# Sums of the hidden quarters rearranged and partly moved from GpSimd to VectorE, with folds at set places, in a Strassen-like channel block beside attention

## The chip, the cores and the metric

The kernel runs on one core of a Trainium2 chip. The metric is the device time of one execution in microseconds (us); lower is better. Three executions of the kernel before took 1725.05 to 1727.2 us, median 1726.35. All runs in this document are in the fast state.

## The reference, cut to what matters

```python
# attention: 8 batches x 8 heads, 576 positions, head dimension 64
scores = q @ k.T / 8
attn = softmax(where(scores >= max(scores) - tau, scores, -1e9))
x = attn @ v                                  # then (batch, 576, 512)
# Fourier mixing and channel block
u  = x + real(fft(fft(x, axis=1), axis=2))
un = (u - mean(u)) / sqrt(var(u) + 1e-6)
out = u + relu(un @ w_ch1) @ w_ch2            # 512 -> 2048 -> 512
```

## The kernel before

TensorE's order is written by hand. Attention's steps and pieces of the channel block alternate on it, so that the block fills the time in which a softmax runs on VectorE and ScalarE. The order of the other engines comes from a scheduler.

The channel block takes 16 groups of 256 tokens "in quarters": each layer is a 2x2 block product in seven products instead of eight, at the price of sums of blocks. The groups alternate between two orders of products, "up" (even) and "down" (odd). For the output layer the hidden activations `h` lie in four quarters `(i, k)`. I write h00, h01, h10, h11, where h01 is `quarter(1, 0)` and h11 is `quarter(1, 1)`, as in the kernel. Each quarter is 128 x 1024 and is worked on in two parts of 512 columns. These are the sums of `h`:

```python
def s_form(out_, in0, in1, op):              # None stands for s_tile
    for part in range(2):
        ...
        nc.gpsimd.tensor_tensor(out=place[0], in0=place[1], in1=place[2], op=op)
...
if up:
    s_form(None, (1, 0), (1, 1), ALU.add)            # s = h01 + h11
    s_form((1, 0), (0, 0), (1, 0), ALU.subtract)     # h01 := h00 - h01
else:
    s_form(None, (1, 0), (1, 1), ALU.add)
    s_form((1, 0), (0, 0), (1, 0), ALU.subtract)
    s_form(None, None, (0, 0), ALU.subtract)         # s := s - h00
sum_ = bank()
yield from product(sum_, a[0][0], b00, True)         # first product: h00
...
yield from fifth() if up else seventh()              # second: s (up) or h00 - h01 (down)
... # third: h10; fourth: s (up: changed once more); then the other three
```

The hidden layer ends with adds and relus; the last of them are in `third` or `fifth`:

```python
def relu(to):
    nc.scalar.activation(out=to, in_=to, func=ACT.Relu)
...                                    # end of a down group, part 1
    add(h01, y)                        # VectorE
    relu(h01)                          # ScalarE
    add(h11, y)
    relu(h11)
```

Beside this, every pair of heads that attention has finished is "folded" for the Fourier transform: two sums `half`, four sums into `f`, two tiny ones, and after some pairs two wide sums. GpSimd folds the first three pairs of a batch, and VectorE the last, whose result the transform of that batch waits for. The program calls one piece of a fold per attention step (`fold_more`).

Names in the profile lines below: `sc` are attention's scores, `neg` their maxima, `e` the exponentials; `pw` and `pe` are TensorE's transposes of `e`, `e_t` and `ends` ScalarE's copies of these; `py` and `pa` are the two products of the Fourier transform, `y_e` the copy of a part of `py`; `ph` and `po` are products of the hidden and the output layer, `hs` is `h`, `s_tile` is s.

Of the kernel before, what the change touches and what calls it, by code (L numbers as in the profile page):

```python
# [12 lines left out]
ALU = mybir.AluOpType  # L13
ACT = mybir.ActivationFunctionType
# [33 lines left out]
def kernel(  # L48
# [12 lines left out]
    nc = tc.nc  # L61
# [109 lines left out]
    for u in range(2):  # L171
# [10 lines left out]
        out=q_scale[:], in0=tau_t[:], scalar1=0.0, scalar2=SCALE, op0=ALU.is_ge, op1=ALU.mult  # L182
# [3 lines left out]
        out=below[:], in0=tau_t[:], scalar1=0.0, scalar2=-3.0e38, op0=ALU.is_lt, op1=ALU.mult  # L186
# [3 lines left out]
        out=tau_pos[:], in0=tau_t[:], scalar1=0.0, scalar2=-1.0, op0=ALU.max, op1=ALU.mult  # L190
# [697 lines left out]
    def hidden_in_quarters(g, rows, quarter):  # L888


        c0 = tokens_of(g)[0] % RING
        c1 = (c0 + 128) % RING
        up = (g - FIRST) % 2 == 0
        b = [[[u_t[:, 2 * k + c, z : z + 128] for c in range(2)] for z in (c0, c1)]
             for k in range(2)]
        t1, t2, minus_t4 = ([t_u[:, m, c, :] for c in range(2)] for m in range(3))

        def sums(out_, in0, in1):
            for c in range(2):
                nc.gpsimd.tensor_tensor(out=out_[c], in0=in0[c], in1=in1[c], op=ALU.subtract)  # L900

        sums(t1, b[0][1], b[0][0])
        sums(t2, b[1][1], t1)
        sums(minus_t4, b[1][0], t2)

        def weights(eng, part, in0, in1, op=ALU.subtract):
            cols = slice(512 * part, 512 * part + 512)
            for c in range(2):
                eng.tensor_tensor(
                    out=s_u[c][:, cols], in0=in0[c][:, cols], in1=in1[c][:, cols], op=op  # L910
                )

        OPERANDS = {
            1: (a_w1[0][0], b[0][0]), 2: (a_w1[0][1], b[1][0]), 3: (s_u, b[1][1]),
            4: (a_w1[1][1], minus_t4), 5: (s_u, t1), 6: (s_u, t2), 7: (a_w1[1][0], b[0][1]),
        }
        banks = {}

        def product(m, part):
            name = "sum" if m in (1, 6, 7) else m  # L920
            if m not in (6, 7):
                banks[name] = ps.tile([128, 512], FP32, tag="mm", bufs=4, name="ph")
            left, right = OPERANDS[m]
            for q in range(4):
                for c in range(2):
                    nc.tensor.matmul(  # L926
                        banks[name][:, 128 * q : 128 * q + 128],
                        left[c][:, 512 * part + 128 * q : 512 * part + 128 * q + 128], right[c],
                        start=q == 0 and c == 0 and m not in (6, 7), stop=c == 1,
                        skip_group_check=True,  # L930
                    )
            return banks[name][:, :]

        def add(to, bank, other=None):
            nc.vector.tensor_tensor(  # L935
                out=to, in0=bank, in1=to if other is None else other, op=ALU.add
            )

        def relu(to):
            nc.scalar.activation(out=to, in_=to, func=ACT.Relu)  # L940

        def fifth(part):
            y = product(5, part)
            h01, h11 = quarter(1, 0, part), quarter(1, 1, part)
            if up:
                nc.scalar.copy(h11, y)

                weights(nc.gpsimd if part else nc.vector, part, s_u, a_w1[0][0])
            else:
                add(h01, y)  # L950
                relu(h01)
                add(h11, y)
                relu(h11)

        def third(part):
            y = product(3, part)
            h01 = quarter(1, 0, part)
            if up:
                add(h01, y)
                relu(h01)  # L960
            else:
                nc.scalar.copy(h01, y)
                weights(nc.gpsimd, part, a_w1[1][1], a_w1[1][0])

        def first(part):
            nc.scalar.copy(quarter(0, 0, part), product(1, part))

        def second(part):
            h00 = quarter(0, 0, part)
            add(h00, product(2, part))  # L970
            relu(h00)

        def others(part):
            h10, h01, h11 = quarter(0, 1, part), quarter(1, 0, part), quarter(1, 1, part)
            x = product(6, part)
            add(h01, x, h11 if up else None)

            if up:
                weights(nc.vector, part, a_w1[0][1], s_u)
            else:  # L980
                weights(nc.vector, part, s_u, a_w1[0][0], ALU.add)
            yield 4096
            nc.scalar.copy(h10, product(4, part))
            yield 4096
            x = product(7, part)
            add(h10, x)
            relu(h10)
            if up:
                add(h11, x)
                relu(h11)  # L990
            else:
                nc.scalar.copy(h11, x)
            yield 4096

        begin, end = (fifth, third) if up else (third, fifth)
        for one in (first, begin) if up else (begin, first):
            one(0)
            yield 4096
        second(0)
        yield 4096  # L1000
        rows.load(1)

        sums(b[0][1], b[1][1], b[0][1])
        yield ND * 128
        yield from others(0)
        begin(1)
        yield 4096
        rows.load(0)
        yield ND * 128
        for one, part in ((first, 1), (second, 1), (end, 0)):  # L1010
            one(part)
            yield 4096
        rows.factors(0, 2)
        yield from others(1)
        end(1)
        yield 4096
# [35 lines left out]
    def channels_in_quarters(g):  # L1052
# [16 lines left out]
        s_tile = sb.tile([128, size], FP32, tag="sums", bufs=1, name="s_tile")  # L1069
        s_sum = tiles(s_tile)  # L1070

        def s_form(out_, in0, in1, op):

            for part in range(2):
                place = [
                    s_tile[:, 512 * part : 512 * part + 512] if at is None else quarter(*at, part)
                    for at in (out_, in0, in1)
                ]
                nc.gpsimd.tensor_tensor(out=place[0], in0=place[1], in1=place[2], op=op)  # L1079

        def product(bank, left, right, start):
            for p in range(NK):
# [10 lines left out]
        def alone(left, right, *to):  # L1093
            po = bank()
            yield from product(po, left, right, True)
            for t, cols in to:
                rows.add(t, cols, po[:, 0 : DM // 2])
            yield 4 * DM
# [6 lines left out]


        if up:
            s_form(None, (1, 0), (1, 1), ALU.add)
            s_form((1, 0), (0, 0), (1, 0), ALU.subtract)
        else:  # L1110
            s_form(None, (1, 0), (1, 1), ALU.add)
            s_form((1, 0), (0, 0), (1, 0), ALU.subtract)
            s_form(None, None, (0, 0), ALU.subtract)
        sum_ = bank()
        yield from product(sum_, a[0][0], b00, True)
        rows.add(0, LEFT, sum_[:, 0 : DM // 2])
# [16 lines left out]
        else:  # L1133
            combine(t_sum_2, b11_2, t_sum_2)
            s_form(None, None, (0, 0), ALU.add)
        yield from alone(a[0][1], b11, (0, RIGHT))
        if up:
            rows.store(0)
        yield from product(sum_, a[1][1], minus_t4, False)
        rows.add(1, LEFT, sum_[:, 0 : DM // 2])  # L1140
        yield 4 * DM
        yield from seventh() if up else fifth()
        if not up:
            rows.store(0)
        rows.store(1)


    mixes = []
# [61 lines left out]
    folds = []  # L1210
# [62 lines left out]
    def fold_more():  # L1273
        if folds and next(folds[0], True):
            folds.pop(0)
# [89 lines left out]
    while folds:  # L1365
        fold_more()

    by_hand.close()
    ctx.enter_context(tc.manual_schedule(engines={mybir.EngineType.PE}))

    for i in range(2 * per_batch, total + 1):
        if i < total:
            scores(i)
            softmax(i)

        n, t = divmod(i, NT)
        fold_more()
        nothing = iter(())
        prep = prep_in_parts(n + 1) if t == 3 and n + 1 < B * NPAIR else nothing
        weights = weights_in_parts(i - 1)  # L1380
        next(prep, None)
        fill()
        next(weights, None)
        fill()
        next(weights, None)
        next(prep, None)
        fill()
        next(prep, None)
        if t == 2:
            weighted_values(n, 0)  # L1390
        if t == 0:
            weighted_values(n - 1, 1)
            folds.append(fold_rows(n - 1))
            if n % NPAIR == 0:
                while folds:
                    fold_more()
            if n + 1 < B * NPAIR:
                load_v(n + 1)
        if i % per_batch == 0:
            start_batch(i // per_batch - 1)  # L1400
# [49 lines left out]
```

## Time and profile before

| | kernel before |
|---|---|
| median of 3 runs | 1726.35 us |
| span of the profiled run | 1723.9 us |
| TensorE busy, whole span | 95% |
| TensorE idle after 430 us, where the groups in quarters run | 48 us of 1294 |
| of that, waits for GpSimd's difference | 14.9 us in three waits |
| clock granted to TensorE after each of these waits | 0.50 for 6.8 us |

TensorE is the bound. What other engines do matters only where TensorE waits for them. A wait costs its idle time and, where the clock record shows a drop after it, half of the busy time at half clock: the eight matmuls of one output product took 3.78 us there (1065.65 us) and 1.89 us at full clock (1058.37 us).

### The profile page before, as it was taken

The numbers are of one execution on the slowest core, as the hardware profiler recorded it, in microseconds if no ns is written. First come the engines' busy times: TensorE is split into PE (matmuls) and PEld (weight loads), VectorE is DVE, ScalarE is ACT, GpSimd is POOL, SyncE is SP. The second block draws the span as 40 slices with busy tenths as digits, with TensorE's granted clock in tenths as the row PEclk, the third lists the DMA queues.
The fourth block names the chain that finished last, engine by engine and source line by source line (L and its number), as shares of the span: only waits on it lengthen the run. The fifth ranks groups of instructions, "written<-read, shape, count | busy, mean of one in ns | idle before, by whom it ended". The sixth has DMA issues, their size and how long they took to land.

```text
span 1723.9 us, 28923 instructions
## 1 busy us (share of the span) xinstructions
PE 1643.3 (95%) x10838; PEld 1282.9 (74%) x10838; DVE 1128.3 (65%) x2470; ACT 844.9 (49%) x1833; POOL 650.8 (38%) x827
## 2 busy tenths in 40 slices
PE   8998899999999999999999998999989998999998
PEld 4555555576886788788889787777868777889998
DVE  6885885566757676856576757685767757663444
ACT  5863675544454454545345455454636455442111
POOL 5773562042421452334351244224232244235343
PEclk9999999999999999999999999999999999999999
DMA  5313222100010001000010010101001010000000
GB/s 160 112 51 106 70 71 54 31 16 21 22 34 19 23 15 41 22 27 20 15 29 27 22 31 4 41 22 34 15 15 40 22 30 5 13 1 13 13 13 13
DMA packets 130384, 57.48 MB, mean 33 GB/s; under 512 B 121123, under 2 KB 121125, under 8 KB 130246
## 3 DMA queue, kind: packets, MB, share of 16 engines
q1 hardware_dynamic: 128854, 55.35, 11.9%
q8 instruction: 86, 1.41, 0.4%
q14 instruction: 52, 0.43, 0.1%
q10 hardware_dynamic: 1392, 0.30, 0.1%
HBM read 46.02 MB, written 9.44 MB: 32 GB/s over the span
## 4 chain that ended last, share of the span: by engine, by line
PE 72%; DVE 13%; ACT 7%; POOL 4%; issue 2%; DMA 1%; SPq 1%; ACTq 0%; DVEq 0%; POOLq 0%
PE ph L926 22%; PE po L1083 18%; PE pv L589 9%; PE sc L433 6%; PE pw L560 5%; PE po L848 3%; ACT e L469 3%; DVE neg L461 3%; DVE e L477 2%; PE sc L444 2%; PE ph L822 1%; PE py L692 1%; DVE hs L1044 1%; DVE f L673 1%; PE pa L709 1%
## 5 line engine op out<-in xcount | busy, mean ns | idle before, releaser
L461 DVE TENSOR_REDUCE neg<-sc 128x1 f32<-128x576 f32 x288 | 205.7, 750 | 201.4 <-PE sc L433 189.4
L469 ACT ACTIVATE e<-sc,neg 128x576 f32<-128x576 f32 x288 | 211.8, 735 | 250.9 <-DVE neg L461 250.2
L477 DVE SCALAR_TENSOR_TENSOR e<-sc,thr,e 128x576 f32<-128x576 f32 x288 | 227.1, 813 | 59.0 <-ACT thr L473 58.1
L1083 PE MATMUL po<-w,hs 128*128 128x256 f32 x1024 | 248.4, 386 | 0.8 <-DVE u L804 0.6
L1083 PEld LDWEIGHTS po<-w,hs 128*128 128x128 f32 x1024 | 187.3, 191 | 34.3 <-issue 11.5
L926 PE MATMUL ph<-u_t,w 128*128 128x128 f32 x1536 | 187.8, 276 | 0.9 <-DVE hs L935 0.7
L560 PE MATMUL pw<-ident,e 128*128 128x128 f32 x1152 | 170.7, 275 | 15.4 <-ACT ends L552 3.2
L926 PEld LDWEIGHTS ph<-u_t,w 128*128 128x128 f32 x1536 | 178.7, 192 | 6.0 <-issue 1.9
L433 PE MATMUL sc<-kT,qT 64*128 64x288 f32 x1024 | 165.9, 429 | 7.9 <-DVE e L477 7.3
L562 ACT COPY e_t<-pw 128x512 f32<-128x512 f32 x256 | 148.2, 592 | 45.6 <-PE pw L560 44.2
L560 PEld LDWEIGHTS pw<-ident,e 128*128 128x128 f32 x1152 | 135.2, 141 | 34.7 <-issue 4.7
L935 DVE TENSOR_TENSOR hs<-ph,hs 128x512 f32<-128x512 f32 x160 | 107.2, 685 | 82.2 <-PE ph L926 58.1
L433 PEld LDWEIGHTS sc<-kT,qT 64*128 64x128 f32 x1024 | 91.4, 186 | 68.4 <-issue 42.1
L804 DVE SCALAR_TENSOR_TENSOR u<-po,rstd,u 128x256 f32<-128x256 f32 (+1 forms) x164 | 76.2, 483 | 85.5 <-PE po L1083 83.6
L926 PE MATMUL ph<-t_u,s_w 128*128 128x128 f32 x1024 | 126.1, 276 | 1.9 <-ACT ends L548 1.1
L926 PEld LDWEIGHTS ph<-t_u,s_w 128*128 128x128 f32 x1024 | 119.3, 192 | 5.8 <-issue 2.3
L1083 PE MATMUL po<-hs,s_tile 128*128 128x256 f32 x512 | 123.1, 384 | 0.0
L940 ACT ACTIVATE hs<-hs 128x512 f32<-128x512 f32 x128 | 79.1, 629 | 70.5 <-DVE hs L935 70.4
L1079 POOL TENSOR_TENSOR s_tile<-hs 128x512 f32<-128x512 f32 x32 | 42.3, 1323 | 171.4 <-ACT hs L940 158.6
L1083 PEld LDWEIGHTS po<-hs,s_tile 128*128 128x128 f32 x512 | 94.1, 191 | 13.8 <-issue 2.1
L496 ACT ACTIVATE e<-e,den 128x576 f32<-128x576 f32 x96 | 74.4, 775 | 53.0 <-DVE den L489 52.4
L1079 POOL TENSOR_TENSOR hs<-hs,s_tile 128x512 f32<-128x512 f32 x32 | 44.8, 1400 | 127.3 <-PE po L1083 122.6
(196 smaller groups left out, 2979.1 us busy)
## 6 DMA issues: line engine op xcount, KB each, us to landing
hs<-in_moe_w_ch_dram SPq DMA_DIRECT2D x23, 512.0 KB, 4.2
out_dram<-u SPq DMA_DIRECT2D x36, 256.0 KB, 2.1
qk_in<-in_q_dram SPq DMA_DIRECT2D x64, 128.0 KB, 2.2
v_in<-in_v_dram SPq DMA_DIRECT2D x64, 128.0 KB, 2.4
qk_in<-in_k_dram SPq DMA_DIRECT2D x31, 128.0 KB, 2.4
w<-in_moe_w_ch_dram SPq DMA_DIRECT2D x6, 512.0 KB, 7.8
qk_in<-in_k_dram SPq DMA_DIRECT2D x31, 64.0 KB, 2.3
stage<-in_moe_w_ch_dram SPq DMA_DIRECT2D x3, 512.0 KB, 3.7
```

The source lines that it names most:

```text
L433: nc.tensor.matmul(sc[j][:, c, 0:HALF], qT[hp, 128 * t : 128 * t + 128], kT[hp, HALF * c : HALF * (c + 1)], start=True, stop=True,)
L461: nc.vector.tensor_reduce(out=neg[:, j : j + 1], in_=sc[j][:, :, 0:HALF], axis=AXIS_XY, op=ALU.max, negate=True,)
L469: nc.scalar.activation(out=ej, in_=sc[j][:, :, 0:HALF], func=ACT.Exp, bias=neg[:, j : j + 1], scale=1.0)
L477: nc.vector.scalar_tensor_tensor(out=ej, in0=sc[j][:, :, 0:HALF], scalar=thr[:, j : j + 1], in1=ej, op0=ALU.is_ge, op1=ALU.mult, accum_out ...
L560: nc.tensor.transpose(pw[:, c, :], e[:, c0 : c0 + 128], ident[:, :])
L562: nc.scalar.copy(e_t[:, 4 * j : 4 * j + 4, qs], pw[:, :, :])
L589: nc.tensor.matmul(pv[64 * j : 64 * j + 64, 0:m], vt[:, 2 * c + j, :], e_t[:, 4 * j + c, 0:m] if c < 4 else ends[:, 0:m], start=(c == 0), ...
L926: nc.tensor.matmul(banks[name][:, 128 * q : 128 * q + 128], left[c][:, 512 * part + 128 * q : 512 * part + 128 * q + 128], right[c], start ...
L935: nc.vector.tensor_tensor(out=to, in0=bank, in1=to if other is None else other, op=ALU.add)
L940: nc.scalar.activation(out=to, in_=to, func=ACT.Relu)
L1079: nc.gpsimd.tensor_tensor(out=place[0], in0=place[1], in1=place[2], op=op)
L1083: nc.tensor.matmul(bank[:, 0 : DM // 2], left[p], right[p], start=start and p == 0, stop=p == NK - 1, skip_group_check=True,)
```

## The change

The intent is to relieve GpSimd at the end of the hidden layer. In down groups the sum is rewritten: s = h01 + h11 - h00 becomes s = h11 - (h00 - h01), so the difference comes first, on VectorE, and one sum less is left. In up groups the first sum goes to VectorE. The last relu of h01 goes from ScalarE to VectorE. Folds are called at set places of the groups.

```diff
-        def relu(to):
-            nc.scalar.activation(out=to, in_=to, func=ACT.Relu)
+        def relu(to, last=False):
+            if last:
+                nc.vector.tensor_relu(to, to)
+            else:
+                nc.scalar.activation(out=to, in_=to, func=ACT.Relu)
...
-                relu(h01)                       # in fifth (down) and third (up)
+                relu(h01, part == 1)
...
+            background()                        # at five places of a group
...
         if up:
-            s_form(None, (1, 0), (1, 1), ALU.add)
+            s_form(None, (1, 0), (1, 1), ALU.add, nc.vector)
             s_form((1, 0), (0, 0), (1, 0), ALU.subtract)
         else:
-            s_form(None, (1, 0), (1, 1), ALU.add)
-            s_form((1, 0), (0, 0), (1, 0), ALU.subtract)
-            s_form(None, None, (0, 0), ALU.subtract)
+            s_form((1, 0), (0, 0), (1, 0), ALU.subtract, nc.vector)
+            s_form(None, (1, 1), (1, 0), ALU.subtract)
...
+    def background():
+        if late:                                # only after the second batch
+            fold_more()
...
-        fold_more()                             # in each step of attention
+        if t > 2:
+            fold_more()
...
+            while folds:                        # in the step that ends a pair
+                fold_more()
```

More of the change, by code (lines that the diff above doesn't have):

```diff
@@ L959, in third @@
                 add(h01, y)
-                relu(h01)
+                relu(h01, part == 1)
             else:
@@ L1003, in hidden_in_quarters @@
         sums(b[0][1], b[1][1], b[0][1])
+        background()
         yield ND * 128
@@ L1011, in hidden_in_quarters @@
             one(part)
+            if one is second:
+                background()
             yield 4096
@@ L1070, in channels_in_quarters, with s_form @@
         s_sum = tiles(s_tile)
-        def s_form(out_, in0, in1, op):
+        def s_form(out_, in0, in1, op, eng=nc.gpsimd):
             for part in range(2):
@@ L1078, in s_form @@
                 ]
-                nc.gpsimd.tensor_tensor(out=place[0], in0=place[1], in1=place[2], op=op)
+                eng.tensor_tensor(out=place[0], in0=place[1], in1=place[2], op=op)
         def product(bank, left, right, start):
@@ L1136, in channels_in_quarters @@
         yield from alone(a[0][1], b11, (0, RIGHT))
+        background()
         if up:
@@ L1140, in channels_in_quarters @@
         rows.add(1, LEFT, sum_[:, 0 : DM // 2])
+        background()
         yield 4 * DM
@@ L1145, in channels_in_quarters @@
         rows.store(1)
+    def background():
+        if late:
+            fold_more()
+    late = []
     mixes = []
@@ L1366 @@
         fold_more()
+    late.append(True)
     by_hand.close()
```

## The prediction

> **What bounds the kernel now.** I read the page first: the busy shares, the slices and the chain that ended last.
>
> ```profile
> PE 1643.3 (95%) x10838; PEld 1282.9 (74%) x10838; DVE 1128.3 (65%) x2470; ACT 844.9 (49%) x1833; POOL 650.8 (38%) x827
> ...
> PE 72%; DVE 13%; ACT 7%; POOL 4%; issue 2%; DMA 1%; SPq 1%; ACTq 0%; DVEq 0%; POOLq 0%
> ```
>
> TensorE is busy 95% of a span of 1723.9 us, so it is the bound, and any gain must come out of its 80.6 us of idle time or out of stretches where it is busy at a lower clock. No other engine is near its limit, so moving work between VectorE, ScalarE and GpSimd is worth only what it changes in TensorE's waits.
>
> The changed lines are executed only by the groups of the channel block "in quarters". The table of stretches puts TensorE at 1245.6 us busy out of 1294 from 430 us (where these groups start) to the end: 48 us idle there, the other 32 us earlier, where the change does nothing. So I asked for TensorE's waits in that window, and for its groups kept apart by form. First the waits (engine, line, whom it waited for: us in total, times, longest), then the group:
>
> ```profile
> PE po L1083 <- POOL hs L1079: 14.9, 3, 5.0
> PE py L692 <- ACT ends L548: 6.5, 4, 2.1
> PE pw L560 <- ACT ends L552: 3.2, 4, 1.3
> PE pw L560 <- ACT y_e L702: 2.9, 1, 2.9
> PE pa L709 <- ACT e_t L564: 2.7, 4, 0.7
> ```
>
> ```profile
> L1083 PE MATMUL po<-hs 128*128 128x256 f32 x256 | 66.4, 407 | 14.9 <-POOL hs L1079 14.9
> ```
>
> A third of the late idle time is three waits of 5 us, all for one thing: the product of the quarter h01 (left) with t_sum, which waits for GpSimd's difference h00 - h01. In every second group (call it "down") that product, the seventh, comes second in the output layer. The timeline of GpSimd around the first of the three (start, us taken, what) shows why:
>
> ```profile
> 1055.41 1.55 POOL L622 TENSOR_TENSOR half<-x 128x287 f32<-128x287 f32 x2
> 1056.91 1.83 POOL L627 TENSOR_TENSOR f<-half 128x143 f32<-128x143 f32 x4
> ...
> 1059.14 1.48 POOL L651 TENSOR_TENSOR sums<-f 128x608 f32<-128x608 f32 x1
> 1060.57 1.72 POOL L1079 TENSOR_TENSOR s_tile<-hs 128x512 f32<-128x512 f32 x1
> 1062.25 1.91 POOL L652 TENSOR_TENSOR f<-f 128x608 f32<-128x608 f32 x1
> 1064.12 1.47 POOL L1079 TENSOR_TENSOR hs<-hs 128x512 f32<-128x512 f32 x1
> ```
>
> The inputs were done at 1054.8 (h01's relu on ScalarE), but GpSimd ran a pair's fold, then the sum that stands before the difference, then the last fold sum, and ended the difference at 1065.6. TensorE stood from 1060.7 to 1065.65. The other two are the same spot one batch later each (1260.02 and 1454.47).
>
> The wait also costs clock. Stretches around it; the column before the DMA share is the granted clock, the first pair after the comma is the length and TensorE's busy time:
>
> ```profile
> 1060.70:1064.30 3.60, 0.00 (x0) 0.00 (x0) 3.60 (x4) 1.25 (x2) 3.60 (x3) 1.00 0.00 0
> 1064.30:1071.10 6.80, 5.45 (x16) 3.53 (x18) 2.35 (x5) 0.00 (x0) 2.52 (x2) 0.50 0.00 0
> ```
>
> After 3.6 us of idle the clock is 0.50 for 6.8 us, of which TensorE works 5.45 us. The two later spots read 5.68 and 5.83 us at 0.50 and 0.51.
>
> **What the Trainium skill says.** "TensorE: Matmul & The Clock Gate", section "What's actually happening": the clock halves after an idle window of about 3.4 us, the windows run freely, and one busy window brings it back. The trace agrees: two windows (6.8 us) at half clock at each of the three spots, whereas the shorter waits for ScalarE cause one window or none. "GPSIMD Engine Reference", section 3.1: an fp32 elementwise op of two inputs is 1.96x slower on GpSimd than on VectorE. Here it is 1323 to 1527 ns against 684 ns (the median of VectorE's sums of weights, 128x512), 1.9 to 2.2x. The same page, section 1, says that the two share SBUF interfaces; the trace agrees: those VectorE sums run from 665 up to 1893 ns, the long ones beside GpSimd work. "VectorE: DVE Perf Modes", section "Mode 2x_2P", lets an op of one SBUF tensor go at two elements a cycle: the 128x576 scaling of e has a median of 520 ns, so I take 0.46 us for a relu of 128x512 (520 x 512/576).
>
> **The change part by part.** There are 16 such groups, 8 "up" and 8 "down"; every sum comes as two instructions.
>
> 1. In down groups s = h01 + h11 (GpSimd) and s = s - h00 (GpSimd) go; h00 - h01 moves to VectorE; s = h11 - (h00 - h01) stays on GpSimd as one sum. In up groups the first sum h01 + h11 moves to VectorE. GpSimd loses 16 + 16 of the first sum (32 x 1.323 = 42.3 us), 16 differences (16 x 1.429 = 22.9), 16 third sums (16 x 1.527 = 24.4) and gets 16 new ones (16 x 1.32 = 21.1): 68.5 us less. VectorE gets 32 sums, 32 x 0.69 = 22 us when nothing disturbs them.
> 2. The last relu of h01 for part 1 moves from ScalarE (16 x 0.629 = 10 us less) to VectorE (16 x 0.46 = 7.4 us more). VectorE goes from 826 to about 856 us of the 1294, 66%.
> 3. The folds are called at other places of the program. I compared the instruction orders of the two builds. TensorE's is identical. On GpSimd, leaving the sums of h aside, it is identical too, fold for fold; VectorE differs there only in that some sums of weights and adds of h have changed places by one to four positions. So the new fold places move nearly nothing by themselves: in the three bad groups the fold still sits on GpSimd at the same place.
>
> What is on the path: in the three bad groups the seventh product now waits only for VectorE. There the last add of h11 ended at 1055.0 and VectorE then idled 1.09 us until the maxima at 1056.09. The relu (0.46) goes in front of that add, which waited 0.35 us for ScalarE's copy anyway, and the difference (0.69) behind it: done at about 1055.8, some 5 us before TensorE wants it at 1060.7, and the maxima are not put off. So each wait disappears whole.
>
> - Idle removed: 14.9 us (3 x 4.95).
> - Half clock removed: busy time at half clock does half the work, so (5.45 + 5.68 + 5.83) / 2 = 8.5 us.
> - Given back: the product of weighted values comes next. It needs ScalarE's copy of the transposed weights, which started at 1061.95 and took 0.56 us, against TensorE's new arrival at about 1062.6. A residue of 0 to 1 us each, say 0.5 x 3 = 1.5 us.
> - The 48 us of other late waits hang on ScalarE behind the softmax; I count no change there.
>
> Sum: 14.9 + 8.5 - 1.5 = 21.9 us; 1726.35 - 21.9 = 1704.5 us.
>
> **Rivals.** (a) The remaining GpSimd sum takes the wait's place: its second half still stands behind the fold's 1.48 us sum. It would end at about 1062, but the product with s_tile is only the fourth, after 1.9 us of the seventh, 2.8 us of weighted values and the whole third product: not before 1067. Against it: 5 us of margin. If it held, half the gain would go: about 1715. (b) VectorE becomes late: 30 us of new work, all at the end of the hidden layer, right before a softmax whose maxima release ScalarE and then TensorE's transposes. For it: the four waits on ScalarE's ends at L692 come from such a chain, and the longest of them, 2.1 us at 732 us, was followed by a half-clock window. Against it: in up groups VectorE idled 3.5 us before its folds, and in down groups the folds on VectorE took 2.0 us for what takes 0.9 us undisturbed, because GpSimd's sums, now gone, ran beside them. 0.5 us in each group would give 8 us back: 1712. (c) The gaps let other engines catch up, so removing them uncovers other waits soon after. Against it: after the gap ScalarE idled 10.1 us and VectorE 3.3 and 2.9 us in turn, which is slack and not debt. It would leave 1710. (d) More than the three: shorter chains and undisturbed VectorE work also shorten the waits for ScalarE, and with them the three single half-clock windows that the trace's clock record has at 538.7, 569.4 and 733.2 us (3.4 us long, so 1.7 us each at most). That would be 1697 to 1700.
>
> **Range and chances.** The three waits are named, equal in every batch, and their new releaser has 5 us of margin, so the bulk seems safe; (b) and (c) pull up, (d) pulls down. Range 1698 to 1712. Faster by over 2% needs 1691.8 or less, 34.5 us: more than the three waits with their clock and all of (d). Slower by 2% would need VectorE to become the bound at 66%.
>
> **What would show it.** Right: the wait of po for GpSimd's hs is gone from TensorE's waits, the clock is 1.0 past 1060 us with no stretch of 6.8 us at 0.50, TensorE's busy time falls by some 8 us and its idle time by some 14; GpSimd falls by about 68 us, VectorE rises by about 30. Wrong: a wait for GpSimd's s_tile or for VectorE's hs at the output products; waits of ScalarE for the maxima that grow so that those of L692 or L560 pass 3.4 us; or the same waits in TensorE with the time unchanged. If the fold places turn out to matter, the folds would stand elsewhere in GpSimd's timeline than at the 1055 us spot.

## The result, and the profile after

The changed kernel takes 1696.97 us (median of 4 runs, 1695.86 to 1699.09). The ratio to the kernel before is 0.9832, with a 95% interval of 0.9815 to 0.9849. Ratios here are the mean time of one kernel's fast runs over that of the other's in the same rounds, so they are not quite the ratio of the medians quoted. The gain is 29.4 us (1726.35 - 1696.97). The prediction was 21.9 us with a range down to 1698.0, so it was too small by 7.5 us and the result lies 1 us outside the range.

The busy shares and the chain on the page of the kernel after:

```profile
PE 1637.6 (96%) x10838; PEld 1280.9 (75%) x10838; DVE 1137.2 (67%) x2518; ACT 835.4 (49%) x1817; POOL 585.6 (35%) x779
...
PE 75%; DVE 13%; ACT 8%; issue 2%; POOL 2%; DMA 0%; ACTq 0%; DVEq 0%; POOLq 0%
```

TensorE has the same number of instructions, GpSimd fell from 4% to 2% of the chain. TensorE's longest waits from 430 us to the end:

```profile
PE py L692 <- ACT ends L548: 5.3, 4, 1.5
PE pw L560 <- ACT ends L552: 3.2, 4, 1.3
PE pa L709 <- ACT e_t L564: 2.7, 4, 0.7
PE pw L560 <- ACT y_e L702: 2.2, 1, 2.2
```

The 14.9 us for GpSimd's `hs` at the output products are gone. The waits at L692 and for `y_e`, which the prediction left as they were, are shorter too.

The stretch from 430 us to the end, in the kernel before and in the kernel after. Columns are the stretch, its length, then the busy time of TensorE's matmuls, its weight loads, VectorE, ScalarE and GpSimd with their instruction counts, then the granted clock and the DMA share with GB/s:

```profile
430.00:1724.00 1294.00, 1245.56 (x8647) 1038.36 (x8645) 826.36 (x1765) 595.36 (x1270) 459.18 (x547) 0.99 0.08 21
```

```profile
430.00:1697.00 1267.00, 1238.59 (x8662) 1036.35 (x8661) 836.23 (x1814) 587.63 (x1258) 395.88 (x500) 1.00 0.08 22
```

TensorE's idle time fell from 48.4 to 28.4 us and its busy time by 7.0 us. GpSimd fell by 63.3 us. VectorE rose by only 9.9 us although it got 48 more instructions (2470 before, 2518 after, on the two pages).

The spot at 1055 us of the kernel before, now in the kernel after. First GpSimd's timeline (start, us taken), then two stretches around TensorE's product:

```profile
1051.16 1.54 POOL L622 TENSOR_TENSOR half<-x 128x287 f32<-128x287 f32 x2
1052.66 1.84 POOL L627 TENSOR_TENSOR f<-half 128x143 f32<-128x143 f32 x4
...
1054.89 1.48 POOL L651 TENSOR_TENSOR sums<-f 128x608 f32<-128x608 f32 x1
1056.33 1.72 POOL L1086 TENSOR_TENSOR s_tile<-hs 128x512 f32<-128x512 f32 x1
1058.00 1.93 POOL L652 TENSOR_TENSOR f<-f 128x608 f32<-128x608 f32 x1
```

```profile
1050.00:1055.70 5.70, 5.70 (x34) 4.70 (x34) 4.91 (x12) 2.84 (x6) 5.54 (x11) 1.00 0.00 0
1055.70:1063.00 7.30, 7.17 (x46) 4.70 (x45) 7.30 (x10) 1.63 (x4) 4.23 (x3) 1.00 0.00 0
```

The fold stands on GpSimd exactly where it stood. Only the difference is no longer in its queue, and TensorE goes on at full clock.

**Where the time went.** TensorE's order is the same in both kernels, so each of its matmuls can be paired with itself in the other trace. The difference of the two start times, stretch by stretch, is a ledger (times of the kernel before; changes between the two profiled runs):

| stretch, us | change, us | what is there |
|---|---|---|
| 0 to 520 | +1.70 | before the change acts: half-clock windows of the start fall elsewhere |
| 520 to 575 | -3.92 | first down group, with a fold on VectorE |
| 575 to 700 | -0.44 | a wait for qT |
| 700 to 740 | -2.87 | second down group, with a fold on VectorE |
| 740 to 950 | -0.95 | small waits |
| 950 to 1000 | +1.67 | a half-clock window that was not there before |
| 1050 to 1080 | -6.90 | first of the three waits |
| 1080 to 1250 | -0.47 | small waits |
| 1250 to 1275 | -6.98 | second of the three |
| 1275 to 1440 | +1.08 | another new half-clock window, less a small wait |
| 1440 to 1470 | -7.03 | third of the three |
| 1470 to end | -1.03 | small waits |

The sum is -26.1 us; another 0.4 us lie after the last matmul. The profiled runs took 1725.68 and 1699.09 us, the latter the slowest of the four. The three waits brought 20.9 us, close to the 21.9 us predicted. The missing 7 us are in the stretches from 520 to 575 and 700 to 740 (together -6.8 us).

### The profile page after: what moved, and what is told of

It is laid out like the page before. It is cut to its first block, busy times and chain, and to the rows that moved or that the text cites. A ratio compares the mean times of both kernels' runs of the same rounds, so it can differ in the third digit from the quotient of the medians.

```text
span 1697.3 us, 28896 instructions
## 1 busy us (share of the span) xinstructions
PE 1637.6 (96%) x10838; PEld 1280.9 (75%) x10838; DVE 1137.2 (67%) x2518; ACT 835.4 (49%) x1817; POOL 585.6 (35%) x779
## 4 chain that ended last, share of the span: by engine, by line
PE 75%; DVE 13%; ACT 8%; issue 2%; POOL 2%; DMA 0%; ACTq 0%; DVEq 0%; POOLq 0%
PE ph L926 23%; PE po L1090 18%; PE pv L589 9%; PE sc L433 7%; PE pw L560 5%; PE po L848 3%; ACT e L469 3%; DVE e L477 3%; DVE neg L461 3%; PE sc L444 2%; PE py L692 1%; PE ph L822 1%; DVE hs L1051 1%; DVE f L673 1%; PE pa L709 1%
## 5 line engine op out<-in xcount | busy, mean ns | idle before, releaser
L943 ACT ACTIVATE hs<-hs 128x512 f32<-128x512 f32 x112 | 69.3, 629 | 70.9 <-DVE hs L935 70.8
L492 DVE TENSOR_SCALAR e<-e,den 128x576 f32<-128x576 f32 x120 | 81.4, 678 | 2.6
```

The costliest lines, as they stand in the source:

```text
L492: nc.vector.tensor_scalar(out=e[:, 0:S], in0=e[:, 0:S], scalar1=den[:, 0:1], scalar2=None, op0=ALU.mult)
```

## The experiments

My theory after reading the traces had two parts. First, the three waits come from the order of the sums in GpSimd's queue. Second, the 7 us come from VectorE's folds in the first two down groups, which GpSimd's sums no longer slow. Rivals: the fold places; the relief of GpSimd and ScalarE as such; VectorE being the faster engine for the difference. All experiments have the kernel before in the same rounds; its median there was 1726.2 to 1726.4 us.

### e1: the fold places alone

```diff
-        fold_more()
+        if t > 2:
+            fold_more()
         # and background() at its places; sums and relu as before
```

> Only the new places of the folds; sums and relu as before. The build has the same instructions in the same order with the same waits on every engine as the kernel before, so my theory expects 1726 us, ratio 1.000 within the noise of 0.2%. Rival (the fold places carry the 7 us that the prediction missed): 0.996 or less.

Measured: 1726.37 us, ratio 1.0003 (0.9991 to 1.0016). This part of the change does nothing: the scheduler gives the same program. The run is therefore also a measure of the noise. Paired with the profiled run of the kernel before it shows +1.72 us before 430 us and then +0.2 us to the end. So the first 430 us of a run differ by luck, and after that a ledger is good to some tenths of a us.

### e2, e3, e4: the other three parts alone

```diff
 # e2: down groups only
+            s_form((1, 0), (0, 0), (1, 0), ALU.subtract, nc.vector)
+            s_form(None, (1, 1), (1, 0), ALU.subtract)
 # e3: up groups only
+            s_form(None, (1, 0), (1, 1), ALU.add, nc.vector)
 # e4: the last relu only
+                relu(h01, part == 1)
```

> Only the sums of the down groups: difference on VectorE, one sum less on GpSimd; folds, up groups and relu as before. Theory: this carries nearly all. The three waits of 4.95 us and their half clock (20.9 us measured by aligning the two traces) and the faster folds on VectorE at the two early down groups (about 7 us) go: 1726 - 21 - 7 = 1698, ratio 0.982 to 0.986. Rival (relief of GpSimd and ScalarE as such brings the 7 us): only the three waits, 1705, ratio 0.988.

> Only the first sum of the up groups on VectorE (16 instructions). Theory: no wait of TensorE hung on it and no fold of VectorE stands beside it at the spots that matter: ratio 0.998 to 1.001. Rival (GpSimd relief as such): its 21 of the 68 us of relief would bring a third of 7 us, ratio 0.9985 or less; VectorE-late rival: 1.001 to 1.003.

> Only the last relu of h01 on VectorE (16 instructions). Theory: ratio 0.998 to 1.001, since the half us it saves ScalarE is not waited for. Rival (ScalarE relief shortens the waits of the transposes for ScalarE, which were 4 of the 7 us): 0.997 or less.

Measured: e2 1697.55 us, ratio 0.9835 (0.9822 to 0.9849); e3 1719.26 us, 0.9964 (0.9951 to 0.9976); e4 1726.12 us, 1.0002 (0.9988 to 1.0016).

The sums of the down groups alone give all of the gain; relu gives nothing. The up sum alone was a miss: 7 us where my theory expected none. On top of the down sums the medians show no gain (1696.97 against 1697.55), but the ledger of the full change against e2 does: steps of 0.45 to 0.7 us, 2.1 us in all, recur where e3 has them (at 640, 1128, 1315 and 1614 us of e2). A half-clock window at 1335.7 us that e2 does not have (1.6 us) and 0.5 us at 727 us take them back. The ledger of e3 against e1 shows two kinds of things. Some 3.3 us are steps of 0.2 to 0.7 us, several of them at waits for VectorE. Another 2.9 us are two half-clock windows that do not come, although the waits before them are still there. The second kind needs a look. In the kernel before, around the wait of 2.09 us at 732 us:

```profile
729.80:733.20 3.40, 1.31 (x9) 1.13 (x9) 3.02 (x9) 2.65 (x6) 2.03 (x2) 1.00 0.00 0
733.20:736.60 3.40, 3.40 (x13) 2.49 (x12) 2.05 (x6) 1.17 (x3) 0.96 (x1) 0.50 0.00 0
```

And in e3, where the same wait of 2.09 us ends at 733.12 us:

```profile
728.20:731.61 3.41, 2.82 (x16) 2.28 (x14) 3.41 (x7) 0.61 (x3) 2.78 (x1) 1.00 0.00 0
731.61:735.03 3.42, 1.91 (x11) 1.76 (x12) 2.96 (x10) 2.97 (x7) 1.33 (x2) 1.00 0.00 0
```

In each of these traces all half-clock windows start on one grid of 3.413 us, and the stretches above are cut on that grid. In the kernel before, the wait lies within one cell and leaves TensorE busy for 1.31 us of it; the next cell has half clock. In e3 the border of two cells cuts the wait, both cells keep 1.9 us or more of work, and nothing follows. So a shift of some tenths of a us makes or removes 1.7 us. That part of e3 is phase and not relief.

### e5, e6: the down sums in some groups only

```diff
-        else:
+        elif g - FIRST < 5:      # e5; in e6: g - FIRST > 5
             s_form((1, 0), (0, 0), (1, 0), ALU.subtract, nc.vector)
             s_form(None, (1, 1), (1, 0), ALU.subtract)
+        else:
+            ...                  # the three sums of before
```

> The new sums only in the first three down groups (those at about 522, 714 and 871 us), the later five as before. Theory: the three waits for GpSimd stay (14.9 us in the waits), the folds on VectorE at the first two groups go from 3.9 and 4.1 us to about 2.1 and 2.5 us, the waits after them and their half-clock windows go: 7 to 8.5 us less, ratio 0.9950 to 0.9962. Rival (the 7 us is luck of the clock windows or load as such): 0.998 to 1.000.

> The new sums only in the last five down groups, among them the three of the waits. Theory: the three waits with their half clock go and nothing else: 21 us less, 1705, ratio 0.9875 to 0.9885. Rival: with the load spread over all groups, 5/8 of the extra 7 us comes too, 1701, ratio 0.985.

The text for e5 miscounts: the condition holds in the first two down groups (at 522 and 714 us); the one at 871 us has the old sums in both kernels.

Measured: e5 1717.75 us, ratio 0.9952 (0.9940 to 0.9965); e6 1704.08 us, 0.9872 (0.9858 to 0.9885). The gains are 8.7 and 22.4 us, together 31, against 28.7 for e2. The 2 us too many fit clock windows: e5 has only one at the first of the three spots (1.1 us), and e2 has one at 959.4 us that costs 1.7 us. In e5 the ledger against e1 has -7.5 us between 520 and 740 us, and the three waits for GpSimd are still 14.8 us. In e6 it has 7.06, 7.14 and 7.16 us at the three spots and next to nothing elsewhere. The gain sits in five groups: two and three. A relief by the down sums that is spread over all groups is excluded.

### e7: the new order, all on GpSimd

```diff
-            s_form(None, (1, 0), (1, 1), ALU.add)
             s_form((1, 0), (0, 0), (1, 0), ALU.subtract)
-            s_form(None, None, (0, 0), ALU.subtract)
+            s_form(None, (1, 1), (1, 0), ALU.subtract)
```

> Down groups with the difference first and one sum less, all still on GpSimd; VectorE, ScalarE, folds, up groups as before. In the build the difference now stands in front of the fold's big sum. Theory: it ends at about the time TensorE wants it (an estimate of 1060 against 1060.7 us), so the three waits go from 4.95 to under 1 us and the half clock with them; one third of the sums beside the early folds go: 1726 - 20 - 3 = 1703, ratio 0.984 to 0.989. Rival (the gain is VectorE being 2x faster than GpSimd and in no queue behind folds): waits of 2 to 4 us stay, ratio 0.992 to 0.998.

Measured: 1699.03 us, ratio 0.9840 (0.9827 to 0.9854). The full change is 0.9832, within noise. GpSimd's timeline in e7 at the first of the three spots, where TensorE takes the second half of the product at 1055.61 us without a wait:

```profile
1050.48 1.55 POOL L622 TENSOR_TENSOR half<-x 128x287 f32<-128x287 f32 x2
1051.98 0.49 POOL L627 TENSOR_TENSOR f<-half 128x143 f32<-128x143 f32 x1
1052.43 1.28 POOL L1086 TENSOR_TENSOR hs<-hs 128x512 f32<-128x512 f32 x1
```

The difference takes 1.28 us on GpSimd and ends at 1053.7, 1.9 us early. VectorE is not needed for the gain at the three spots (7.9 to 8.0 us each in the ledger): it is enough that no other sum has to come before the difference, so that the scheduler can put it ahead of the fold's wide sum. No run has the difference first and still three sums, so the order and the smaller number of sums are told apart by this timeline only. From 430 us on the ledger puts e7 4.0 us behind the full change (one half-clock window more, and steps of 0.5 to 0.9 us elsewhere); the medians, 2.1 us apart, do not resolve that.

### e8: the old order, the difference on VectorE

```diff
             s_form(None, (1, 0), (1, 1), ALU.add)
-            s_form((1, 0), (0, 0), (1, 0), ALU.subtract)
+            s_form((1, 0), (0, 0), (1, 0), ALU.subtract, nc.vector)
             s_form(None, None, (0, 0), ALU.subtract)
```

> Down groups with the three old sums in the old order, only the difference on VectorE. It overwrites h01, so it must wait for GpSimd's first sum, which stands behind the fold's sum, and VectorE stands in front of the softmax's maxima meanwhile. Theory (order, not engine): waits of about 2 us stay at the three spots, without half clock, VectorE idle up to 7 us before the difference: 15 to 18 us less, ratio 0.989 to 0.992. Rival (engine alone is enough): as the full change, 0.984.

Measured: 1725.74 us, ratio 0.9996 (0.9983 to 1.0008). The engine alone brings nothing, and not even the half that I expected. VectorE's timeline in e8 at the first spot (in brackets the idle time before and who ended it), then TensorE's:

```profile
1061.28 1.93 DVE L1086 TENSOR_TENSOR hs<-hs 128x512 f32<-128x512 f32 x1 [6.87 <-POOL s_tile L1086]
1063.14 1.41 DVE L461 TENSOR_REDUCE neg<-sc 128x1 f32<-128x576 f32 x2
```

```profile
1065.74 1.12 PE L560 MATMUL pw<-ident,e 128*128 128x128 f32 x4 [6.07 <-ACT ends L548]
1066.65 3.62 PE L1090 MATMUL po<-hs 128*128 128x256 f32 x8
```

In VectorE's order the difference stands before the maxima, and VectorE stood 6.87 us before it until GpSimd had read h01. The maxima came at 1063.1. ScalarE's exponentials wait for the maxima, its copy of `ends` stands behind the exponentials, and TensorE's transposes wait for that copy: 6.07 us in place of 4.95. I had expected the late softmax to be hidden; I had overlooked that copy. The wait changed its releaser and its place, and the time stayed.

### e9: VectorE's folds disturbed again

```diff
 # edit of the full change
-            s_form(None, (1, 1), (1, 0), ALU.subtract)
+            for _ in range(3 if g - FIRST < 5 else 1):
+                s_form(None, (1, 1), (1, 0), ALU.subtract)
```

> The full change, but in the first two down groups (at about 522 and 714 us) GpSimd writes its one sum three times over, with the same values each time; nothing waits for the repeats there. Theory (the 7 to 8 us of those two groups are VectorE's folds, slowed by GpSimd sums beside them): the halves go back from 0.53-0.71 to about 1.0 us and the sums of the fold from 0.30 to about 0.56 us each, the maxima come 1.3 to 2 us later, and the waits for ScalarE with their half-clock windows return: 1697 + 5 to 8 = 1702 to 1705, ratio 0.986 to 0.988. Rival (order of the sums, or the number of waits, not contention): 1697 to 1698, ratio 0.983.

Measured: 1702.62 us, ratio 0.9862 (0.9847 to 0.9877), 5.65 us more than the full change. The order on all other engines is that of the full change. VectorE's two groups of folds from 500 to 760 us, in the kernel before, in the full change and in e9 (count, busy us, mean ns of one, then idle time before and its releaser):

```profile
L622 DVE TENSOR_TENSOR half<-x 128x287 f32<-128x287 f32 x4 | 4.0, 1031 | 3.7 <-ACT x L595 3.7
L627 DVE TENSOR_TENSOR f<-half 128x143 f32<-128x143 f32 x8 | 4.0, 563 | 0.0
```

```profile
L622 DVE TENSOR_TENSOR half<-x 128x287 f32<-128x287 f32 x4 | 2.7, 707 | 1.5 <-ACT x L595 1.5
L627 DVE TENSOR_TENSOR f<-half 128x143 f32<-128x143 f32 x8 | 1.9, 295 | 0.0
```

```profile
L622 DVE TENSOR_TENSOR half<-x 128x287 f32<-128x287 f32 x4 | 5.1, 1306 | 1.3 <-ACT x L595 1.3
L627 DVE TENSOR_TENSOR f<-half 128x143 f32<-128x143 f32 x8 | 4.0, 563 | 0.0
```

One repeat follows the other while VectorE folds, and the folds are slower even than before the change: 5.1 + 4.0 us, against 4.0 + 4.0 before and 2.7 + 1.9 in the full change. The maxima come 5.04 and 5.25 us after the start of their scores in the two groups (4.51 and 4.68 before, 2.64 and 3.11 in the full change). The ledger against the full change has +2.83 us between 520 and 545 us, +3.23 us between 700 and 740 us, and -1.67 us for a half-clock window at 960 us that did not come: +4.4 us from 430 us on. (Before 430 us, where the two do the same, e9's profiled run was 4.0 us luckier, so the profiled runs as wholes look alike.) TensorE's wait for `y_e` is back at 2.9 us (2.2 in the full change) and the longest at L692 at 2.1 (1.5). No wait of TensorE for GpSimd came with the repeats. This shows the second part of the theory: GpSimd's sums slow VectorE's folds, the maxima come late, and TensorE waits for ScalarE behind them.

### e10: an attempt at the longest remaining wait

```diff
 # edit of the full change
-                    nc.scalar.copy(y[0:n, u, 256:257], py[0:n, 0:1])
+                    nc.vector.tensor_copy(y[0:n, u, 256:257], py[0:n, 0:1])
```

> The full change, and the copy of one column of y_e (24 instructions) moved from ScalarE to VectorE. It stood behind two exponentials, and TensorE's longest remaining wait (2.18 us at 537 us) hung on it, with a half-clock window after it. Theory: the wait shrinks to under 1 us and the window goes, 2 to 4 us less: 1693 to 1695, ratio 0.980 to 0.982. Rival (the next thing on ScalarE, the copy of ends behind the same exponentials, takes its place, as at L692): 1696 to 1698, ratio 0.983.

Measured: 1702.22 us, ratio 0.9865 (0.9848 to 0.9881), slower than the full change by 5 us. Neither theory had that. From e10's waits of TensorE:

```profile
PE pw L560 <- DVE y_e L702: 6.4, 5, 1.7
```

The copy now stands in VectorE's queue, and TensorE waits for it there, five times in place of once. In return its waits at L692 for `ends` fell from 5.3 to 0.8 us, so the wait changed its place and stayed. From 430 us on, the ledger against the full change adds up to only +0.4 us. The other +2.0 us lie before 430 us; the copies of the first batches moved too, but the start also differs by luck from run to run, and I did not separate the two. The profiled run of the full change was its slowest, so this comparison also leaves 3 us of the medians unexplained.

## Why the prediction was right or wrong

**The three waits: right.** They went whole, and the ledger has 6.90 + 6.98 + 7.03 = 20.9 us against the 21.9 us predicted. By subtraction, 2.5 us (23.4 - 20.9) were given back or never lost, in place of 1.5. e6 shows the three spots by themselves.

**VectorE in time for the difference: right in this build, and for a reason that the prediction did not see.** It named the queue and counted on the engine. e7 shows that GpSimd is early enough too if the difference stands first; e8 shows that VectorE is not if it stands second. The cause is the rewritten sum, which frees the difference of its predecessor.

**The step that failed** is the one that reads "The 48 us of other late waits hang on ScalarE behind the softmax; I count no change there". (48 us is the whole idle time from 430 us on; without the three waits it is 33.5 us.) They hang on ScalarE, ScalarE on VectorE's maxima, and the maxima stood behind folds that GpSimd's sums slowed. The prediction had the numbers in its rival (b): folds of 2.0 us "for what takes 0.9 us undisturbed". It used them only as an argument that VectorE would not be late, not as a gain. That term of the sum was 0 and measured 6.8 us in the full change, 7.5 us in e5, and 6.1 us came back in e9. The maxima in the first such group came 1.9 us sooner after the scores: 526.38 us against the scores' start at 521.87 before, 526.20 against 523.56 after. Scores, fold and maxima there, before and after:

```profile
521.87 1.24 PE L433 MATMUL sc<-kT,qT 64*128 64x288 f32 x8
522.47 1.90 DVE L622 TENSOR_TENSOR half<-x 128x287 f32<-128x287 f32 x2 [2.05 <-ACT x L595]
524.29 2.02 DVE L627 TENSOR_TENSOR f<-half 128x143 f32<-128x143 f32 x4
...
526.38 1.41 DVE L461 TENSOR_REDUCE neg<-sc 128x1 f32<-128x576 f32 x2
```

```profile
523.56 1.24 PE L433 MATMUL sc<-kT,qT 64*128 64x288 f32 x8
524.16 1.10 DVE L622 TENSOR_TENSOR half<-x 128x287 f32<-128x287 f32 x2 [0.99 <-ACT x L595]
525.19 0.95 DVE L627 TENSOR_TENSOR f<-half 128x143 f32<-128x143 f32 x4
...
526.20 1.41 DVE L461 TENSOR_REDUCE neg<-sc 128x1 f32<-128x576 f32 x2
```

**Rival (d)** was therefore the one that held. Its size, 1697 to 1700 us, just reached the result, but I gave it too little weight, and the low end of 1698 cut it off. With the term at 6.8 us the sum would have been 1726.35 - 21.9 - 6.8 = 1697.6 us. That this meets the median so well is partly luck: two new half-clock windows (+3.2 us together) and small waits that shrank elsewhere (-3.4 us) happen to cancel. Of (d)'s three windows one stayed (now at 537.0 us).

**The Trainium skill on this point.** "SBUF — State Buffer", section "Who interferes with whom", says that a VectorE instruction with two SBUF inputs contends with a GpSimd instruction that reads SBUF. I had not drawn on it for the folds. The runs agree: two `half` sums take 1031 ns each beside GpSimd's three sums (kernel before) and 525 ns in e2, and e9 puts the disturbance back.

**VectorE's load: wrong in size.** About 30 us more were predicted and 9.9 us came. The new instructions cost 11.7 + 11.5 + 7.7 = 30.9 us on VectorE (sums of 730 and 719 ns, relus of 479 ns, close to the 690 and 460 estimated). So some 21 us went elsewhere on VectorE. From 430 us on, its sums of first-layer weights fell from 69.4 to 59.2 us, those of second-layer weights from 111.3 to 107.7, the folds' six sums per pair from 15.3 to 11.7 and the scaling of e from 76.5 to 74.7: 19.2 us, with the same counts and shorter instructions.

**GpSimd and TensorE: right.** GpSimd fell by 63.3 us (68 predicted), TensorE's busy time by 7.0 us (8). Its idle time fell by 20.0 us where 14 were predicted; of the 6 us more, 3.1 us are the shorter waits of (d) in the first two down groups, and the rest are small changes elsewhere.

**The fold places: right.** They move nothing; e1 is the same program.

**Relu and up sum.** The prediction gave them no part in the gain. e2 reaches the full gain without them. Alone, the up sum gives 7 us (e3), a part of which is phase of the clock windows; with the down sums about 2 us of it stay in the ledger, and a new window and 0.5 us elsewhere hide them.

Left open is which windows of half clock come in a given build: they moved by 1 to 2 us in most runs, and I can read them from a trace but did not predict them.

## What to carry to other kernels

When one engine waits for a result of another, look first at what stands ahead of it in the queue and whether algebra can make the wanted result come first; a faster engine behind the same predecessor gained nothing here (e8). When instructions leave GpSimd, also count what VectorE gains beside them, and follow that gain through the chain to the bound engine. Where TensorE waits, count its idle time and the half clock after it.

## What the Trainium skill lacked or had wrong

- "TensorE: Matmul & The Clock Gate", sections "What's actually happening" and "Why this matters for your kernels", gives an idle window of about 3.4 us, and gaps over about 3 us, as what halves the clock (it speaks of frequent small gaps too, without a measure). Here shorter waits did: cells of the 3.41 us grid in which TensorE was still busy for 1.31 us (before, 729.8 to 733.2 us), 1.44 us and 1.66 us (full change, before 537.0 and 960.3 us) were followed by half clock. Cells with 1.91 us (e3) and 2.12 us (full change, 1144.7 to 1148.1 us) were not. Over all twelve traces from 430 us on, cut on each trace's grid, every cell at full clock with less than 1.65 us of work was followed by half clock and none with more than 1.75 us, about half a cell. A cell that is itself at half clock can have more and be followed by another: 2.04 us before, 1064.28 to 1067.69 us. Before 430 us there are exceptions both ways (2.03 us followed at 103.5 us in the full change, 1.43 us not at 230.3 us in e9), which stay open. The prediction called its trace in agreement with the page; the single windows after waits of about 2 us in it already did not fit. So a wait of 1.5 us, with smaller ones around it, can cost 1.7 us more, and the same wait of 2.09 us cost it or not by where it lay on the grid.
- "SBUF — State Buffer", section "Who interferes with whom", says that VectorE and GpSimd block each other but has no measured price for sums of two inputs on both (it gives a 6.8x and a 1.5x without the operations). Here VectorE's fold sums took 1031 and 563 ns beside GpSimd's sums, and 525 and 295 ns without most of them.
- No page that I found gives the time by which the start of a run varies: an identical program (e1) differed by 1.72 us before 430 us, with half-clock windows in other places, and by 0.2 us in the 1290 us after it.
